# Value tiles of 96 rows, split over 8 DMA engines instead of 16

## The chip, the cores and the metric

The kernel runs on one core of a Trainium2 chip. The core has a matrix engine (TensorE, PE in the profile, with its weight loads as PEld), VectorE (DVE), ScalarE (ACT), GpSimd (POOL) and SyncE (SP), which here issues the DMAs, and 16 DMA engines that carry them out. What counts is the time of one launch on the device in microseconds (us), as the median of several runs.

## The reference

Four sequences of 768 tokens with 8 heads of 64 pass through windowed attention with summaries, and the result through a layer with a gate:

```python
k_sum = k.reshape(B, H, nb, block, D).max(axis=3)        # block 32: 24 summaries
v_sum = v.reshape(B, H, nb, block, D).mean(axis=3)
mask_l = np.abs(pos[:, None] - pos[None, :]) < window     # window 16
scores_l = scale * (q @ k.T)                              # masked by mask_l
scores_s = scale * (q @ k_sum.T) + np.log(block)
a = softmax(concatenate([scores_l_masked, scores_s]))
x = a @ concatenate([v, v_sum])                           # tokens x 512
h = x @ w_in                                              # 512 -> 2048
out = (h * erf(softplus(h))) @ w_out                      # 2048 -> 512
```

All inputs and the output are float32.

## The kernel before, in words

The 3072 tokens are six chunks of 512. A chunk and a pair of heads make a *quad*, 24 in all. For attention a quad is cut into eight blocks of 64 queries; a block needs 96 keys and values around it and the 24 summaries of its sequence, so a block's product of probabilities and values runs over 120 rows: the 96 rows of a value tile, and 24 rows of value summaries below them. The value tile of a quad is `vw`, [120 rows, 8 blocks, 128 columns]; its 96 rows come by one DMA from the DRAM array `v_win` (a row is 8 x 128 floats, 4096 bytes, 384 KB in all), and its other 24 rows by a DMA from the tile `vsum`, where the summaries lie once. The product is called px in the profile (line 663, function `av`).

The gated layer is cut into 24 periods, six chunks by four groups of hidden columns. In each period TensorE makes h for one group (`mm1`, in later periods `products`, which saves multiplications by sums of blocks of the weights), ScalarE and VectorE make softplus, erf and the gate, and `mm2` adds the group's part of the output. Products are made in pieces of a rounded high part and a low part, which need three passes. The attention of later quads is placed between them: `load_quad` brings queries and keys, `load_quad_v` the value tile, about a period before `av` uses it.

The first chunk is special. Its four quads (pairs 0 to 3) have value tiles of their own, `vwf`, two pairs in one buffer, loaded by `load_vw_first` (line 493), and the rows of the summaries come from `vsum_first`: pair 0's by a copy on ScalarE, pairs 1 to 3 by DMAs (line 510). Between these loads SyncE issues the first weight loads `rw` (line 314, 1024 KB each), which VectorE converts from 64-bit to 32-bit floats. TensorE fills some gaps there with products of zeros (`idle`, line 958), a fixed number of them.

What sets the order: the program adds every piece of work to a plan with its engine, an assumed duration and what it reads and writes. `P.order` then runs the plan through once, with a table `TUNE` of added numbers by piece, and so writes down a fixed order for each engine. All loads are SyncE's. A DMA gets one of eight completion semaphores in turn, and SyncE doesn't issue a DMA before the one that is eight before it on that semaphore has landed; it also waits for whoever last used the buffer.

On the host, `kernel` cuts the windows of the values out of `v` and lays them down as `v_win`, [6 chunks, 4 pairs, 96 rows, 8 blocks, 128 columns]. What is done on the host isn't part of the time.

Of the kernel before, what the change touches and what calls it, by code (L numbers as in the profile page):

```python
# [23 lines left out]
NP = H // 2  # L24
T = 512
SB = S // 64
NB = T // 64
# [3 lines left out]
LW = 96  # L31
NK = LW + NS
NCH = B * S // T
# [147 lines left out]
def bfloat16(x):  # L181

    n = np.array([x], np.float32).view(np.uint32)
    return float(((n + 0x8000) & 0xFFFF0000).astype(np.uint32).view(np.float32)[0])
# [3 lines left out]
def block_attention_mlp(ctx: ExitStack, tc: tile.TileContext, q_t, k_nat, k_win, v_tok, v_nat, v_win, w_in, w_out, out):  # L188
    nc = tc.nc
# [7 lines left out]
    def sb(shape, dtype, name, tag=None):  # L197

        n = math.prod(shape[1:])
        if n % 128 == 0:  # L200
            return pool.tile(shape, dtype, name=name, tag=tag or name)
        t = pool.tile([128, -(-n // 128) * 128], dtype, name=name, tag=tag or name)[0:shape[0], 0:n]
        return t if len(shape) == 2 else t.rearrange("p (a b) -> p a b", a=shape[1]) if len(shape) == 3 else t.rearrange("p (a b c) -> p a b c", a=shape[1], b=shape[2])
# [31 lines left out]
    for i in range(3):  # L235
        c = bfloat16(rest)
# [37 lines left out]
    def dma(kb, fn, r=(), w=(), hold=2.0, **kw):  # L274
        return P.add({"SP": max(0.45, kb / 350.0)}, lambda e: fn(), r, w, hold=hold, **kw)
# [196 lines left out]

    st = {}

    def where(qd):

        ch, p = divmod(qd, NP)
        seqs = {}
        for j in range(NB):
            seqs.setdefault((NB * ch + j) // SB, []).append(j)  # L480
        return ch, p, [(b, slice(js[0], js[-1] + 1)) for b, js in seqs.items()]
# [8 lines left out]
            dma(786, lambda n=n: nc.sync.dma_start(out=vts[n], in_=v_tok[3 * n:3 * n + 3].rearrange("t s c -> s t c")), w=[f"vt{n}"])  # L490

    def load_vw_first(p):
        dma(585, lambda: nc.sync.dma_start(out=st[p]["vw"][0:LW], in_=v_win[0, p]), w=[f"vwf{p}"])

    def ksum_first(p):
        on({"DVE": 0.86}, lambda e: e.tensor_reduce(ksum[:, 0, p], groups(kfirst[p]), op=ALU.max, axis=AX.X), [f"kf{p}"], [f"ksum0{p}"])
# [16 lines left out]
    def load_quad(qd):  # L513
        ch, p, seqs = where(qd)
        s = st[qd] = {}

        def go_q():
            s["qb"] = sb([128, T], F32, "qb")
            nc.sync.dma_start(out=s["qb"], in_=q_t[ch, p])

        def go_k():
            s["kw"] = sb([128, NB, NK], F32, "kw")
            nc.sync.dma_start(out=s["kw"], in_=k_win[ch, p])
        dma(262, go_q, w=["qb"])
        dma(465, go_k, w=["kw"])
        for b, js in seqs:
            n = js.stop - js.start
            on({"DVE": 0.06 + 0.025 * n, "ACT": 0.2 + 0.018 * n}, lambda e, b=b, js=js, n=n: copy(e, s["kw"][:, js, LW:NK], ksum[:, b % 2, p:p + 1, :].to_broadcast([128, n, NS])),
               [f"ksum{b % 2}{p}"], ["kw"])

    def load_quad_v(qd):
        ch, p, seqs = where(qd)
        s = st[qd]

        def go():
            s["vw"] = sb([NK, NB, 128], F32, "vw")
            nc.sync.dma_start(out=s["vw"][0:LW], in_=v_win[ch, p])
        dma(585, go, w=["vw"])
        for b, js in seqs:
            n = js.stop - js.start  # L540
            dma(100 if n == NB else 50, lambda b=b, js=js, n=n: nc.sync.dma_start(out=s["vw"][LW:NK, js], in_=vsum[vrows[b % 2], p:p + 1, :].to_broadcast([NS, n, 128])),
                [f"vsum{b % 2}{p}"], ["vw"])
# [422 lines left out]
    for p in range(NP):  # L965
        load_vw_first(p)
# [69 lines left out]
    for k in range(NPER):  # L1036
        qa, qs = k + NP, k + NP + 1
        ch, g = divmod(k, NG)
# [169 lines left out]
```

## Time and profile before

| | |
|---|---|
| median of 3 runs | 622.92 us (621.27 to 622.95) |
| profiled execution, its own time | 622.58 us |
| its span, first to last instruction | 620.8 us |
| TensorE busy | 612.9 us, 99% |
| VectorE, ScalarE busy | 424.0 us, 422.3 us (68% each) |
| granted TensorE clock | 1.000 |
| DMA | 150.25 MB in 36845 packets, mean 242 GB/s |
| of it v_win | 24 tiles of 384 KB |

The page cuts the span into 40 slices of some 15.5 us and gives the busy share of each engine in tenths:

```profile
PE   9999999999999999999999999999999999999997
DVE  4989999975989886766857646548546556425442
DMA  8999868654784698799767776756786654574612
GB/s 321 256 337 354 287 205 283 250 183 172 247 304 184 236 339 309 244 370 319 240 217 245 234 264 232 257 209 216 266 289 219 225 170 181 210 265 162 246 68 69
```

TensorE reads 9 in nearly all slices; the DMA engines' 9s are in the first few. A busy TensorE is not the same as a full one, and filling products with zeros count as busy too. In the views that follow, a row of the chain or the timeline begins with the start and the length in us; a row of waits names the engine and line that waited, what it waited for, the sum in us, how often, and the longest.

### The profile page before, as it was taken

The page shows a single profiled execution, that of the slowest core. Times are in us where ns is not written, and L with a number is a line of the kernel's source. Part 1 is how long each engine was busy: PE and PEld are TensorE (multiplying, and loading weights), DVE is VectorE, ACT ScalarE, POOL GpSimd, SP SyncE. Part 2 cuts the span into 40 slices and gives each one's busy share as a digit, 9 for nine tenths or more (in the row PEclk, how much of TensorE's full clock was granted, in tenths as well). Part 3 has the DMA queues.
Part 4 walks back from the last instruction along what each step waited for, and adds up shares of the span by engine and source line. Part 5 has one row for each costly group of instructions (what it writes and reads, how often), then busy time and mean ns, then how long its engine had stood idle before and what let it go on. Part 6 is the DMA issues. An engine that isn't in the chain of part 4 may idle for free.

```text
span 620.8 us, 12141 instructions
## 1 busy us (share of the span) xinstructions
PE 612.9 (99%) x4786; PEld 514.4 (83%) x4786; DVE 424.0 (68%) x884; ACT 422.3 (68%) x855; POOL 3.7 (1%) x27
## 2 busy tenths in 40 slices
PE   9999999999999999999999999999999999999997
PEld 5676666888788889989889889899898898899886
DVE  4989999975989886766857646548546556425442
ACT  5869988986879786885866854855756655552450
POOL 2000000000000000000000000000000000000000
PEclk9999999999999999999999999999999999999999
DMA  8999868654784698799767776756786654574612
GB/s 321 256 337 354 287 205 283 250 183 172 247 304 184 236 339 309 244 370 319 240 217 245 234 264 232 257 209 216 266 289 219 225 170 181 210 265 162 246 68 69
DMA packets 36845, 150.25 MB, mean 242 GB/s; under 512 B 3956, under 2 KB 9396, under 8 KB 24244
## 3 DMA queue, kind: packets, MB, share of 16 engines
q1 hardware_dynamic: 36212, 148.95, 69.4%
q8 instruction: 38, 0.62, 0.4%
q10 hardware_dynamic: 576, 0.52, 0.2%
q14 instruction: 19, 0.16, 0.1%
HBM read 124.13 MB, written 23.07 MB: 237 GB/s over the span
## 4 chain that ended last, share of the span: by engine, by line
PE 93%; DMA 6%; SPq 0%; issue 0%; DVE 0%; ACT 0%
PE ops L921 39%; PE hb L807 15%; PE h L766 13%; PE ha L807 11%; PE ops L917 4%; PE px L663 4%; PE pA L566 3%; DMA rw<-w_in 2%; DMA vwf<-vsum 2%; PE pA L637 1%; PE pB L637 1%; DMA vt<-v_tok 1%; PE pB L566 0%; PE vt L460 0%; SPq L485 0%; SPq L486 0%
## 5 line engine op out<-in xcount | busy, mean ns | idle before, releaser
L921 PE MATMUL ops<-w,gh 128*128 128x512 f32 x704 | 232.8, 396 | 0.0
L921 PEld LDWEIGHTS ops<-w,gh 128*128 128x128 f32 x704 | 132.5, 188 | 27.9 <-issue 0.6
L921 PE MATMUL ops<-w,gl 128*128 128x512 f32 x352 | 137.3, 390 | 0.0
L1166 ACT ACT_TABLE_LOAD x87 | 111.6, 1283 | 1.5
L897 DVE TENSOR_TENSOR hc<-wt,hc 128x1024 f32<-128x1024 f32 x44 | 53.3, 1220 | 76.5 <-ACT wt L885 76.5
L766 PE MATMUL h<-xh,w 128*128 128x512 f32 x256 | 88.8, 406 | 0.0
L278 ACT COPY hc<-hb 128x256 f32<-128x256 f32 x61 | 22.7, 373 | 96.2 <-DVE hc L860 47.6
L921 PEld LDWEIGHTS ops<-w,gl 128*128 128x128 f32 x352 | 66.3, 188 | 12.0
L606 ACT ACTIVATE pr<-pr,stats 128x120 f32<-128x120 f32 x160 | 60.9, 383 | 0.2
L766 PEld LDWEIGHTS h<-xh,w 128*128 128x128 f32 x256 | 48.1, 188 | 12.3 <-issue 2.1
L807 PE MATMUL hb<-w,ws 128*128 128x256 f32 x384 | 56.3, 283 | 0.0
L904 DVE TENSOR_TENSOR gl<-hc,gh 128x1024 fp32r<-128x1024 f32 x44 | 53.8, 1222 | 1.6 <-ACT gh L278 0.7
L807 PEld LDWEIGHTS hb<-w,ws 128*128 128x128 f32 x384 | 50.7, 192 | 0.1
L885 ACT ACTIVATE wt<-wt 128x1024 f32<-128x1024 f32 x48 | 50.4, 1061 | 0.4
L766 PE MATMUL h<-xl,w 128*128 128x512 f32 x128 | 49.9, 390 | 0.0
L857 DVE TENSOR_TENSOR hc<-hb,hc 128x256 f32<-128x256 f32 x32 | 13.5, 422 | 37.4 <-PE hb L807 36.4
L278 DVE CAST gh<-hc 128x1024 fp32r<-128x1024 f32 x38 | 26.3, 691 | 18.1 <-PE ops L921 17.1
L873 ACT ACTIVATE wt<-hc 128x1024 f32<-128x1024 f32 x32 | 32.4, 1052 | 0.2
L606 ACT ACTIVATION_READ_ACCUMULATOR pr<-pr,stats 128x1 f32 x160 | 30.0, 187 | 0.0
L917 PE MATMUL ops<-a32s,gw 128*128 128x512 f32 x64 | 29.5, 595 | 0.0
L766 PEld LDWEIGHTS h<-xl,w 128*128 128x128 f32 x128 | 24.1, 188 | 5.6 <-issue 1.2
L807 PE MATMUL ha<-w,ws 128*128 128x256 f32 x192 | 28.3, 283 | 0.0
(162 smaller groups left out, 1033.9 us busy)
## 6 DMA issues: line engine op xcount, KB each, us to landing
w<-dr SPq DMA_DIRECT2D x36, 1024.0 KB
ws<-ds SPq DMA_DIRECT2D x30, 1024.0 KB
kw<-k_win SPq DMA_DIRECT2D x20, 480.0 KB
rw<-w_in SPq DMA_DIRECT2D x8, 1024.0 KB
rw<-w_out SPq DMA_DIRECT2D x8, 1024.0 KB
dr<-w SPq DMA_DIRECT2D x8, 1024.0 KB
ds<-ws SPq DMA_DIRECT2D x8, 1024.0 KB
vw<-v_win SPq DMA_DIRECT2D x20, 384.0 KB
```

The lines of the kernel that those rows point to most:

```text
L278: e.copy(o, i) if e is nc.scalar else e.tensor_copy(o, i)
L606: nc.scalar.activation(s["pr"][:, j], s["pr"][:, j] if qd >= MQ else s["sc"][j // NI][:, i * NK:(i + 1) * NK], AF.Exp, scale=-1.0 if qd >= ...
L663: nc.tensor.matmul(xo[r, o], lhsT=s["vw"][:, j, r], rhs=s["pt"][:, a, o], start=True, stop=True)
L766: nc.tensor.matmul(hs[k, f][:, 0:T], lhsT=w[m], rhs=xt[ch, cc][x], start=(cc == 0 and n == 0), stop=(cc == 3 and n == 2))
L807: nc.tensor.matmul(shape, lhsT=w[m], rhs=y[l], start=first and c == 0 and i == 0, stop=c == 1 and i == 2, skip_group_check=True)
L873: nc.scalar.activation(wt[k, n], hc[k, n], AF.Softplus)
L885: act(0.96, lambda n=n: nc.scalar.activation(wt[k, n], wt[k, n], AF.Erf, scale=-1.0 if k < SOFT else 1.0), [s], [s], table=("sig",), after ...
L897: e.tensor_tensor(hc[k, n], wt.pop((k, n)), hc[k, n], op=ALU.mult)
L904: e.tensor_tensor(gs[k, n][1], hc.pop((k, n)), f32(gs[k, n][0]), op=ALU.subtract)
L917: nc.tensor.matmul(os_[ch, t], lhsT=x[0][:, i % 2, t * 128:(t + 1) * 128], rhs=w32["o", g, i // 2][:, i % 2], start=first, stop=last)
L921: nc.tensor.matmul(os_[ch, t], lhsT=x[y][:, i % 2, t * 128:(t + 1) * 128], rhs=w[m], start=first and n == 0, stop=last and n == 2)
L1166: nc.scalar.preload_act_table_set(sets[o["load"]])
```

## The change

The 96 rows of a tile lie in DRAM as 8 groups of 12 rows, and after each group there is room for a thirteenth row that is never read. The source of the DMA thus has the three sizes 8, 12 and 1024 instead of 96 and 1024, and can't be joined into one run of 96 rows. The destination in the chip's memory, the bytes, the length of a row and the place in SyncE's order are the same. All 24 loads of `v_win` are changed, the four of the first chunk and the twenty of the others. The first size, 8, is what is meant to set over how many DMA engines a transfer is split.

```diff
+    def eight(ch, p):
+        return v_win[ch, p, :, 0:12].rearrange("e r (j c) -> e r j c", c=128)
...
     def load_vw_first(p):
-        dma(585, lambda: nc.sync.dma_start(out=st[p]["vw"][0:LW], in_=v_win[0, p]), w=[f"vwf{p}"])
+        dma(585, lambda: nc.sync.dma_start(out=st[p]["vw"][0:LW], in_=eight(0, p)), w=[f"vwf{p}"])
...
             s["vw"] = sb([NK, NB, 128], F32, "vw")
-            nc.sync.dma_start(out=s["vw"][0:LW], in_=v_win[ch, p])
+            nc.sync.dma_start(out=s["vw"][0:LW], in_=eight(ch, p))
...
-    v_win = np.ascontiguousarray(windows(v).transpose(0, 2, 4, 1, 3, 5)).reshape(NCH, NP, LW, NB, 128)
+    v_win = np.zeros((NCH, NP, 8, 13, NB * 128), dtype=f)
+    v_win[:, :, :, :12] = windows(v).transpose(0, 2, 4, 1, 3, 5).reshape(NCH, NP, 8, 12, NB * 128)
```

## The prediction

> **What bounds the kernel now.** I read first the page's busy line, then stretches of the span, then TensorE's own waits, then the chain that ended last, and last the queue of DMAs in the stage that these left over. The page and two rows of the stretches (busy time of PE, PEld, DVE, ACT, POOL, then the granted clock, DMA share, GB/s):
>
> ```profile
> PE 612.9 (99%) x4786; PEld 514.4 (83%) x4786; DVE 424.0 (68%) x884; ACT 422.3 (68%) x855; POOL 3.7 (1%) x27
> 0.00:40.00 40.00, 35.57 (x485) 23.56 (x486) 28.96 (x48) 26.45 (x91) 3.69 (x27) 1.00 0.97 287
> 40.00:100.00 60.00, 60.00 (x384) 39.59 (x385) 59.11 (x109) 51.68 (x92) 0.00 (x0) 1.00 0.83 293
> ```
>
> TensorE is busy in 60.00 of the 60.00 us from 40 on, at the full clock (1.00); the 4.4 us that it misses early lie in the first 40 us, where the DMA engines are busy 0.97 of the time. So the kernel has two parts: a start bound by DMA, and a rest bound by TensorE. TensorE's waits and the chain (start, length, what) agree:
>
> ```profile
> PE px L663 <- DMA vwf<-vsum: 2.1, 2, 1.1
> PE px L663 <- ACT prf L626: 0.5, 1, 0.5
> PE px L663 <- issue: 0.4, 1, 0.4
> ...
> 2.60 7.28 DMA vt<-v_tok
> 9.90 15.35 DMA rw<-w_in
> 25.26 14.56 DMA vwf<-vsum
> 39.83 0.14 issue
> 39.97 1.15 PE px L663 x32
> ```
>
> The chain runs through DMAs up to 39.83 and through TensorE from 39.97. That last px (pair 3's product with the value tile) needs pair 3's 96-row v_win tile and the 24-row copy from vsum that is issued behind it. After it no px waits for a value tile: the rows above are all the waits that a px has, and none names vw.
>
> **The queue of the start.** These are SyncE's issues of the four v_win tiles and of pair 3's copy, and the weight loads (rw, 1024 KB) between them:
>
> ```profile
> 6.42 0.43 SPq L314 DMA_DIRECT2D rw<-w_in  x1
> 7.59 0.34 SPq L493 DMA_DIRECT2D vwf<-v_win  x1
> 9.90 0.34 SPq L314 DMA_DIRECT2D rw<-w_in  x1
> 10.89 0.33 SPq L493 DMA_DIRECT2D vwf<-v_win  x1
> 21.82 0.52 SPq L314 DMA_DIRECT2D rw<-w_in  x1
> 22.39 0.42 SPq L493 DMA_DIRECT2D vwf<-v_win  x1
> 22.86 0.43 SPq L314 DMA_DIRECT2D rw<-w_in  x1
> 23.33 0.81 SPq L493 DMA_DIRECT2D vwf<-v_win  x1
> 25.26 0.83 SPq L510 DMA_DIRECT2D vwf<-vsum  x1
> ```
>
> All four tiles stand ahead of the copy that lands at 39.83, 14.56 us after its issue. The queue is backed up, so what an engine carries for the tiles delays everything behind them. The rate in stretches:
>
> ```profile
> 10.00:15.00 5.00, 4.92 (x79) 2.86 (x79) 2.50 (x7) 4.01 (x24) 0.00 (x0) 1.00 1.07 417
> 15.00:20.00 5.00, 4.96 (x82) 2.90 (x81) 4.97 (x11) 4.94 (x28) 0.00 (x0) 1.00 1.02 292
> 20.00:25.00 5.00, 4.55 (x53) 3.17 (x52) 5.00 (x9) 4.95 (x20) 0.00 (x0) 1.00 1.06 233
> 25.00:30.00 5.00, 3.95 (x50) 3.08 (x49) 4.96 (x7) 2.80 (x5) 0.00 (x0) 1.00 1.02 257
> 30.00:35.00 5.00, 4.48 (x48) 3.55 (x46) 3.89 (x7) 3.87 (x11) 0.00 (x0) 1.00 1.03 281
> 35.00:40.00 5.00, 3.97 (x28) 3.09 (x24) 3.98 (x5) 2.61 (x4) 0.00 (x0) 1.00 1.02 277
> 40.00:45.00 5.00, 5.00 (x49) 4.08 (x50) 4.97 (x6) 2.86 (x5) 0.00 (x0) 1.00 1.02 409
> 23.00:27.00 4.00, 3.54 (x33) 2.67 (x32) 3.96 (x6) 3.88 (x15) 0.00 (x0) 1.00 1.09 159
> 34.00:38.00 4.00, 3.99 (x49) 3.59 (x50) 2.94 (x4) 2.41 (x4) 0.00 (x0) 1.00 1.04 243
> ```
>
> With the engines always busy, tiles of 128 rows come at 417 and 409 GB/s, but the 25 us in which 96-row and 24-row tiles run among them come at a mean of 268 (292, 233, 257, 281, 277). By bytes 25 x (1 - 268/417) = 8.9 us are lost there. I take this as tiles of other row counts getting in the way of their neighbours; the trace shows the rate, not the cause.
>
> **The change, part by part.** Nothing on TensorE, VectorE, ScalarE or GpSimd is added or moved, and the order of SyncE's issues stays.
>
> (1) *The split itself.* How many engines take part shows in the small packets, one per engine and DMA:
>
> ```profile
> DMA packets 36845, 150.25 MB, mean 242 GB/s; under 512 B 3956, under 2 KB 9396, under 8 KB 24244
> w<-dr SPq DMA_DIRECT2D x36, 1024.0 KB
> ...
> vw<-vsum SPq DMA_DIRECT2D x12, 96.0 KB
> vw<-vsum SPq DMA_DIRECT2D x16, 48.0 KB
> vwf<-vsum SPq DMA_DIRECT2D x3, 96.0 KB
> ```
>
> The view lists 255 DMAs; 255 x 16 = 4080, and 4080 - 3956 = 124 = 31 x 4, so the 31 copies of 24 rows run on 12 engines and all others on 16. The split follows the leading size, so 8 groups should give 8. I expect 24 x 8 = 192 small packets fewer, 3764.
>
> (2) *Four tiles in the start.* A tile is 384 KB: 24,576 bytes an engine now, 49,152 on each of eight engines then. The extra 24,576 bytes take 0.94 us at the full rate (417/16 = 26.1 GB/s an engine) and 1.47 us at the stage's (268/16 = 16.8). Four tiles stand ahead of pair 3's copy: +3.8 to +5.9 us. The other eight engines get ahead by as much, but a landing waits for the last engine, and what they then find queued is what stands behind the tiles. The earlier px at 27.90 and 34.01 move by part of this sum; they are not added, since the last one contains them.
>
> (3) *What the smaller spread gives back.* Only eight engines write a 96-row tile at a time, so there may be less of the 8.9 us loss. The copies from vsum aren't touched: 23 to 27 us, where they run, loses 4 x (1 - 159/417) = 2.5 us alone, and half of the 1.7 us of 34 to 38 is likewise theirs. At most some 5.6 us are the v_win tiles'. The ends are then 3.8 - 5.6 = -1.8 and +5.9 us. I take +3.8: the full-rate price, with the loss neither smaller nor larger. For a change in the loss there is no row that shows it, and twelve rows on eight engines keep as many rows of the tile beside the other engines' weight rows, only for longer.
>
> [...]
>
> (4) *Who pays.* TensorE ends its work ahead of pair 3's px soon after the last row here that precedes it, and then idles:
>
> ```profile
> 27.90 1.15 PE L663 MATMUL px<-ptr,vwf 120*64 120x64 f32 x32 [1.05 <-DMA vwf<-vsum]
> 34.01 1.15 PE L663 MATMUL px<-ptr,vwf 120*64 120x64 f32 x32 [0.52 <-ACT prf L626]
> 38.55 0.39 PE L766 MATMUL h<-xh,w 128*128 128x512 f32 x1
> 39.97 1.15 PE L663 MATMUL px<-ptr,vwf 120*64 120x64 f32 x32 [1.03 <-DMA vwf<-vsum]
> ```
>
> So there is no slack in front of a later landing: the px starts 0.14 us after it. And with TensorE fully busy from 40 us on there is none behind: every microsecond goes to the end. VectorE waits for weight loads in this stage too (row below); those land later by fewer tiles, so its shift is smaller than the px's and is hidden behind it.
>
> ```profile
> DVE a L331 <- DMA rw<-w_in: 2.1, 2, 1.0
> L541 SPq DMA_DIRECT2D vw<-vsum x28: 785/827/883, 63.0 to 499.7; - x28
> L537 SPq DMA_DIRECT2D vw<-v_win x20: 328/337/728, 53.6 to 494.3; - x20
> ```
>
> (5) *The issue.* The new pattern has a size more than the old, like the copies', whose issue takes 827 ns where a v_win issue takes 337. Per tile that is 0 to +0.49 us on SyncE. I take 0: the tiles at 22.39 and 23.33 are queued behind work of many microseconds. Uncovered, four would cost 2.0 us.
>
> (6) *Twenty later tiles.* Each is slower by 0.94 to 1.47 us on its engines. I take 0, covered by TensorE's work: no px waits for vw. Uncovered, all twenty would cost up to 29 us; one alone, 1.5.
>
> The profiled execution's time is 622.58 us with a span of 620.8, so 1.8 lie around it; it is 0.34 under the median, 622.92. The sum is 622.58 + 3.8 = 626.4, or **626.7** against the median.
>
> **The rivals.** *No measurable change*: the loss shrinks by about what the eight engines carry more, 1.9 to 5.6 us, and the copy lands between 1.8 us earlier and 1.9 us later: 621.1 to 624.8. The dips in the rate speak for it, the untouched vsum copies against it. In this I also count that the DMAs still run on 16 engines, against the count of small packets: 622.9.
>
> *Larger loss*: the eight engines meet neighbours as often per byte as now. From 15.0 us an engine carries four rw (65,536 each), four tiles and three copies (8,192 each), 385,024 bytes, 14.8 us at the full rate, and takes 24.8 (to 39.83), a factor 1.68. With 483,328 bytes: 18.5 x 1.68 = 31.1 us, 6.3 later: 629.2. For it speaks that the slow stretches hold nearly the whole stage; against it, fewer engines in the tile.
>
> *Faster*: the v_win tiles stop disturbing the weight loads altogether, and TensorE's waits before px go: 1.05 + 0.52 + 1.03 and the 0.4 of issue, 3.0 us at most: 619.9. It decides from the point where pair 3's copy lands before 38.0 us. Against it: the second of these waits belongs to ScalarE, and the 5.6 us would have to go entirely.
>
> *A late tile in the TensorE part*: a px after 40 us begins to wait for vw, 1 to 2 us for each that does, on top of the forecast: 628 to 630. Against it stands that no such wait exists now.
>
> **How the numbers follow.** Forecast (a landing 1.9 to 5 us later, 624.8 to 628): 0.41. Larger loss 0.19; no measurable change 0.28, of which 0.03 for no split; faster 0.07; a late tile 0.05. A measurement of this kernel tells 0.3%, 1.87 us, from no change: 621.05 to 624.79 is the same. So slower 0.65, same 0.28, faster 0.07. The range leaves out the faster case, the early edge of the no-change case and the worst of the larger loss: 621.7 to 630.0; the forecast's own is 624.8 to 628.
>
> **What would show it.** The split: 3764 packets under 512 B. Term 2: the last px on vwf starts near 43.8 instead of 39.97, with a wait of some 4 to 5 us for DMA vwf. Term 3: the rate from 15 to 40 us; near 268 GB/s or a little under bears the forecast out, over 300 the no-change or the faster case. Term 4: busy 60.00 of 60.00 after the shifted px. Term 5: the issue of v_win near 827 ns. Term 6: no row of a px waiting for vw. I am wrong if the copy lands before 41.7 us, or if the end moves by other than the last px does.

## The result, and the profile after

Over 14 runs each, the kernel after takes 624.8 us in the median (622.97 to 630.25) and the kernel before 622.34 (621.11 to 623.23). The ratio is 1.0056, with an interval from 1.0036 to 1.0076: slower by 3.5 us, with 2.2 to 4.7 as bounds. The ratio is that of the means (625.72 and 622.22 us); the medians lie only 2.5 us apart, since six of the 14 runs after are over 626 and pull the mean up. The profiled execution takes 627.37 us with a span of 625.6, which is 4.8 more than the span before, so it lies on the upper side of the runs. What follows is used for where the time goes; how much goes is taken from the runs.

The page after, its busy line and its packets:

```profile
PE 615.0 (98%) x4786; PEld 516.0 (82%) x4786; DVE 424.7 (68%) x884; ACT 422.0 (67%) x855; POOL 3.7 (1%) x27
DMA packets 36653, 150.25 MB, mean 240 GB/s; under 512 B 3764, under 2 KB 9204, under 8 KB 24052
```

The same instructions and the same bytes; 192 small packets fewer (3956 before), as one per engine and DMA gives when 24 tiles go from 16 engines to 8. TensorE's products of pairs 0 to 3 with their value tiles, in order of time (start, length, what, and in brackets how long TensorE stood idle ahead of it and for what):

```profile
22.15 1.62 PE L666 MATMUL px<-ptr,vwf 120*64 120x64 f32 x32
28.42 1.15 PE L666 MATMUL px<-ptr,vwf 120*64 120x64 f32 x32 [1.31 <-DMA vwf<-vsum]
37.11 1.98 PE L666 MATMUL px<-ptr,vwf 120*64 120x64 f32 x32 [3.08 <-DMA vwf<-v_win]
44.74 1.15 PE L666 MATMUL px<-ptr,vwf 120*64 120x64 f32 x32 [1.16 <-DMA vwf<-vsum]
```

Before, the last three started at 27.90, 34.01 and 39.97. The lag is 0.52, then 3.10, then 4.77 us: it grows from tile to tile, and what it is at the last of them is what the span is longer by. A wait that did not exist before has the largest part, pair 2's product waiting for its own 96 rows. The chain of waits names the same place; its last DMA is pair 3's copy, issued at 24.81 and landed at 44.61 (before: 25.26 and 39.83).

```profile
24.81 19.80 DMA vwf<-vsum
```

Stretches of the kernel after (busy us of PE, PEld, DVE, ACT, POOL, then the granted clock, the DMA share, GB/s):

```profile
20.00:25.00 5.00, 4.85 (x56) 3.55 (x56) 5.00 (x10) 4.92 (x19) 0.00 (x0) 1.00 0.75 238
25.00:30.00 5.00, 3.59 (x48) 2.49 (x46) 5.00 (x7) 2.73 (x8) 0.00 (x0) 1.00 1.05 264
30.00:35.00 5.00, 4.02 (x18) 2.98 (x16) 2.96 (x7) 4.40 (x12) 0.00 (x0) 1.00 1.03 258
35.00:40.00 5.00, 2.89 (x37) 2.81 (x38) 2.70 (x4) 0.88 (x2) 0.00 (x0) 0.71 1.02 278
15.00:40.00 25.00, 20.32 (x234) 14.55 (x233) 20.62 (x32) 17.91 (x66) 0.00 (x0) 0.94 0.97 267
45.00:100.00 55.00, 55.00 (x320) 35.83 (x319) 52.57 (x88) 47.81 (x85) 0.00 (x0) 1.00 0.75 271
```

Two things are new. From 20 to 25 us the DMA engines are busy 0.75 of the time, where before they were busy throughout (1.06). And from 35 to 40 the granted clock is 0.71. What is not new is the rate over the whole stretch from 15 to 40 us: 267 GB/s after, 268 before. From 45 us on TensorE is busy without a gap (575.00 of the 575.00 us to 620), and no px waits for a later value tile.

### The profile page after: what moved, and what is told of

Its sections match the earlier page's. It is cut to its first block, busy times and chain, and to the rows that moved or that the text cites. A ratio compares the mean times of both kernels' runs of the same rounds, so it can differ in the third digit from the quotient of the medians.

```text
span 625.6 us, 12141 instructions
## 1 busy us (share of the span) xinstructions
PE 615.0 (98%) x4786; PEld 516.0 (82%) x4786; DVE 424.7 (68%) x884; ACT 422.0 (67%) x855; POOL 3.7 (1%) x27
## 2 busy tenths in 40 slices
DMA packets 36653, 150.25 MB, mean 240 GB/s; under 512 B 3764, under 2 KB 9204, under 8 KB 24052
## 4 chain that ended last, share of the span: by engine, by line
PE 94%; DMA 3%; ACT 1%; SPq 1%; DVE 0%; issue 0%
PE ops L924 39%; PE hb L810 15%; PE h L769 13%; PE ha L810 11%; PE ops L920 4%; PE px L666 4%; DMA vwf<-vsum 3%; PE pA L569 3%; PE pA L640 1%; PE pB L640 1%; ACT prf L609 1%; PE idle L961 1%; PE pB L569 0%; PE vt L460 0%; SPq L513 0%; SPq L496 0%
## 5 line engine op out<-in xcount | busy, mean ns | idle before, releaser
L278 ACT CAST xh<-px 128x512 fp32r<-128x512 f32 (+1 forms) x17 | 8.9, 524 | 32.1 <-PE px L666 28.8
```

The lines of the kernel that those rows point to most:

```text
L278: e.copy(o, i) if e is nc.scalar else e.tensor_copy(o, i)
```

## The experiments

The theory (A) was the prediction's: in the start the eight engines that carry a v_win tile carry twice its bytes, four such tiles stand ahead of pair 3's copy, and the last px and the end move by that. Its rivals: (B) the later twenty tiles cost something; (C) the pattern itself costs, its gaps or its issue; (D) fewer engines at one tile give something back. The changed line numbers of variants are those of their own code. "Faster" and "slower" are against the kernel before, run on the same chip.

### Which tiles: the first four, or the later twenty

Both lay the DRAM tile out as 104 rows. One kernel reads the gapped form for chunk 0 alone; the other, with `False` in place of `True`, for all chunks but 0. The edit of the host's part, which fills the rows to match, is left out here:

```
-        return v_win[ch, p, :, 0:12].rearrange("e r (j c) -> e r j c", c=128)
+        if (ch == 0) == True:
+            return v_win[ch, p].rearrange("(e r) x -> e r x", r=13)[:, 0:12].rearrange("e r (j c) -> e r j c", c=128)
+        return v_win[ch, p, 0:LW].rearrange("r (j c) -> r j c", c=128)
```

> Only the four value tiles of the first chunk lie in 8 groups of 12 rows; the other twenty are read as 96 rows, as before. Theory A (the start): the eight engines' extra rows ahead of pair 3's copy set the end, the later tiles are covered by TensorE. It expects the whole loss here: +2.5 to +4.5 us against before, the last px on vwf at 42.5 to 45, 3956 - 32 = 3924 packets under 512 B. Theory B (the later tiles cost, by disturbing the weight loads or by a late vw) expects less than half of it, under +1.7 us.

> The other part alone: the four first tiles are read as 96 rows, the twenty later ones in 8 groups. Theory A (the start) expects no change, within 1 us of before, the last px on vwf near 40 and no px that waits for vw. Theory B (the later tiles) expects +1.7 us or more. Packets under 512 B: 3956 - 160 = 3796.

With the first four alone: 625.91 us, a ratio of 1.0057 (1.0036 to 1.0079), which is the whole loss of the change. With the later twenty alone: 622.27 us, 0.9998 (0.9986 to 1.0009). The products of pairs 1 to 3 in the one, and then pair 3's in the other:

```profile
29.16 1.98 PE L668 MATMUL px<-ptr,vwf 120*64 120x64 f32 x32 [2.57 <-DMA vwf<-vsum]
37.52 1.15 PE L668 MATMUL px<-ptr,vwf 120*64 120x64 f32 x32
43.47 1.15 PE L668 MATMUL px<-ptr,vwf 120*64 120x64 f32 x32 [1.02 <-DMA vwf<-vsum]
```

```profile
40.02 1.15 PE L668 MATMUL px<-ptr,vwf 120*64 120x64 f32 x32 [0.97 <-DMA vwf<-vsum]
```

Pair 3's product starts 3.5 us later than before in the one, with a span 3.5 longer (624.3 against 620.8), and at 40.02 with the span of before (620.8) in the other. Which of the earlier products takes the longest wait differs between the two traces (pair 1's here, pair 2's in the kernel after); the lag at pair 3 is what counts. B falls: whatever the twenty tiles cost on their engines (0.94 us each and more by the prediction's estimate) vanishes behind TensorE's work.

### How many engines: 16, 12, 8, 4

The same gapped layout with other group sizes; the function `eight` reads rows `0:6`, `0:8` or `0:24` of a group instead of `0:12`:

```
-    v_win = np.zeros((NCH, NP, 8, 13, NB * 128), dtype=f)
-    v_win[:, :, :, :12] = ...reshape(NCH, NP, 8, 12, NB * 128)
+    v_win = np.zeros((NCH, NP, 16, 7, NB * 128), dtype=f)      # or 12, 9 / 4, 25
+    v_win[:, :, :, :6] = ...reshape(NCH, NP, 16, 6, NB * 128)  # or 12, 8 / 4, 24
```

> All 24 tiles lie in 16 groups of 6 rows with a gap of one row: the pattern with three sizes, the gaps and the longer issue stay, the number of engines goes back to 16. Theory A (rows per engine in the start) expects no change, within 1 us of before, and 3956 packets under 512 B. Theory C (the pattern, the gaps or the issue of about 0.74 us instead of 0.34 cost the time, not the number of engines) expects the whole loss, +2.5 to +4.5 us.

> All 24 tiles lie in 12 groups of 8 rows, so that 12 engines take 8 rows each, two more than before. Theory A (rows of the busiest engine ahead of pair 3's copy): 4 tiles x 2 rows x 4096 bytes at 26.1 to 16.8 GB/s, +1.3 to +2.0 us. [...] Packets under 512 B: 3956 - 24 x 4 = 3860.

> All 24 tiles lie in 4 groups of 24 rows, so that four engines take 24 rows each, 18 more than before instead of 6. Theory A says that the loss goes with the rows of the busiest engine: 4 tiles x 18 rows x 4096 bytes at 26.1 GB/s is +11.3 us, at the slow rate of the stage (16.8 GB/s) +17.6; it expects +9 to +14 us, the last px on vwf at 49 to 54. Theory D (the loss comes from collisions on the way into the 96 rows, which become fewer the fewer engines write) expects less than twice the loss with 8 groups, under +6 us. Packets under 512 B: 3956 - 24 x 12 = 3668.

Small packets were 3956, 3860 and 3668, so these tiles ran on 16, 12 and 4 engines. The price by the forecast's term is the bytes that the busiest engine carries more over four tiles, at the 26.1 GB/s that each moved from 10 to 15 us before (417/16):

| engines | rows on the busiest | bytes more, four tiles | at 26.1 GB/s | measured (interval) |
|---|---|---|---|---|
| 16, with gaps | 6 | 0 | 0 | +0.1 us (-0.7 to +0.9) |
| 12 | 8 | 32,768 | 1.3 us | +0.6 us (-0.6 to +1.7) |
| 8 (the change) | 12 | 98,304 | 3.8 us | +3.5 us (2.2 to 4.7) |
| 4 | 24 | 294,912 | 11.3 us | +13.4 us (12.5 to 14.5) |

The first row takes C away: the gaps and the additional size of the pattern cost nothing that can be measured. The twelve-engine run does not decide between A and no price at all; its profiled execution (624.8 us of span, px of pair 3 at 43.95) was at the upper end of its runs, which go from 620.94 to 626.58. The last row is the largest effect of the study, and it is where the term says, in the waits for value tiles:

```profile
33.06 1.97 PE L666 MATMUL px<-ptr,vwf 120*64 120x64 f32 x32 [5.57 <-DMA vwf<-vsum]
42.51 1.15 PE L666 MATMUL px<-ptr,vwf 120*64 120x64 f32 x32 [1.70 <-DMA vwf<-v_win]
51.53 1.97 PE L666 MATMUL px<-ptr,vwf 120*64 120x64 f32 x32 [4.08 <-DMA vwf<-vsum]
```

In this trace pair 3's product starts 11.56 us later than before (51.53 against 39.97), next to the 11.3 of the term. The span is 13.0 us longer, so 1.4 us are lost behind that product, where the granted clock was 0.50 until about 54.9 us. So the measured loss, with an interval from 12.5, lies above 11.3, but the lag at the last product is the term's; what is lost behind it was not in the forecast.

D falls as an explanation of the total: no layout was faster than 16 engines. The rates are against it too. From 15 to 40 us the twelve-engine kernel moved 245 GB/s, less than the 268 of the kernel before, while 16 groups of six rows moved 301:

```profile
20.00:25.00 5.00, 4.60 (x56) 3.36 (x55) 5.00 (x10) 4.95 (x20) 0.00 (x0) 1.00 0.82 189
15.00:40.00 25.00, 22.56 (x270) 16.50 (x270) 23.75 (x35) 19.20 (x65) 0.00 (x0) 1.00 0.98 301
```

That row says one thing more: 33 GB/s above the kernel before in the mean of this stretch, and no gain in the time (+0.1 us). The rate of a stretch is not the landing that is waited for. The packet counts give how many engines a DMA ran on (16, 12, 8 and 4, and 12 for the 24-row copies). That four such tiles meet the same engines each time, as the sum of the term takes it, was the author's estimate; no row here shows which engines they were, but the prices in the table fit a sum over four tiles.

### Does the clock make it worse?

After the wait of 3.08 us the granted clock was 0.50 for some 3.4 us (37.1 to about 40.5), and the px itself took 1.98 us instead of 1.15. To see what that costs, the four-engine kernel, where the waits are longest, was given products with a zero operand ahead of the products of pairs 1 to 3, so that TensorE never stood idle for long:

```
-FILL = {30: 3, 48: 2, 79: 1, 81: 6, 93: 5, 91: 1, 111: 1}
+FILL = {30: 3, 48: 2, 79: 1, 81: 6, 93: 5, 91: 1, 111: 1, 86: 22, 95: 8, 104: 15}
```

> The kernel with 4 groups of 24 rows (635.56 us), with products of zeros put ahead of px 1, 2 and 3 (22, 8 and 15 of them, some 0.22 us each), so that TensorE does not sit idle there. In the run without them the granted clock was 0.50 for 3 to 3.5 us after the waits of 5.57 and 4.08 us, and the span grew by 13.0 us although the last px moved by 11.6. If the lower clock costs the difference, the clock stays at 1.00 and the time falls by 1 to 2 us, to 633.5 to 634.5. If the wait alone counts, the time stays at 635.6 or grows.

```profile
51.53 1.15 PE L666 MATMUL px<-ptr,vwf 120*64 120x64 f32 x32 [1.07 <-DMA vwf<-vsum]
```

The product takes 1.15 again and the mean clock is 1.00, but it starts at the same 51.53, and the time is 635.45 us against 635.56. The expectation of a gain was wrong: up to the last px, work at half the clock was finished before the next tile landed anyway. The span of this one execution is 0.8 us shorter, all of it behind the last px, but the medians of four runs each do not show it.

With eight engines no such run was made, but the clock is not the whole loss there either. Of the 14 runs after, two had a mean clock of 1.000 and took 624.05 and 624.83 us, 1.8 and 2.6 us over the mean of the kernel before. The six runs over 626 us all had 0.997 or less. Whether the lower clock makes those longer, or only comes with longer waits, is not shown.

### Is it SyncE, held at the copies?

The dip to 0.75 suggested another theory. SyncE issues its DMAs in order, and stands at the first copy from vsum until vsum is there, at about 20.4 us (a wait of 8.9 us); the weight loads of the start wait behind it, the next of them until 22.18 us. With 16 engines the queue of the kernel before held enough for all (1.06); with eight, the engines without v_win rows may have run dry, so that what the others carry could not be covered. A row above already speaks against it: the kernel with 16 groups had a dip too, to 0.82 in the same five microseconds, and no loss. If the theory were true, the loss would go when the copies leave SyncE's queue. This theory is H. First GpSimd made the copies itself, in the kernel before and in the kernel after:

```
-                dma(100, lambda p=p: nc.sync.dma_start(out=st[p]["vw"][LW:NK], in_=vsum[LW:NK, p:p + 1, :].to_broadcast([NS, NB, 128])), ...)
+                dma(100, lambda p=p: copy(nc.gpsimd, st[p]["vw"][LW:NK], vsum[LW:NK, p:p + 1, :].to_broadcast([NS, NB, 128])), ...)
```

> The kernel before (96 rows on 16 engines), but the three copies of 24 rows from vsum into the first value tiles are made by GpSimd, which is idle, instead of by DMAs; the orders of the other engines stay. If the copies cost the queue what the prediction took from the rate (2.5 us at 23 to 27 us and some 0.8 later), the last px on vwf comes earlier, up to what TensorE's waits allow: -1 to -2.6 us, with a rate from 15 to 40 us near 300 GB/s. SyncE also no longer waits there for vsum, which works the same way. If the slow rate is the 96-row tiles' alone, within 1 us of before and a rate near 268.

> The same copies by GpSimd, with the tiles in 8 groups of 12 rows. If the copies' cost and the eight engines' rows simply add, the loss of the changed kernel shrinks by some 3 us: -1 to +1 us against before. If the eight engines' rows alone set the landing of the last tile, the loss stays: +2 to +4 us, and the last px waits for v_win itself.

With 16 engines 623.15 us, a ratio of 1.0012 (1.0000 to 1.0024); with eight 623.32, 1.0016 (1.0007 to 1.0026). So the loss of the eight engines is all but gone, 0.2 us between the two. But three things had changed at once: SyncE is free, the three DMAs are gone, and VectorE is slower while GpSimd works beside it. GpSimd's copies and one of VectorE's instructions under them, and then the same instruction in the kernel before:

```profile
20.34 3.50 POOL L278 COPY vwf<-vsum 24x1024 f32<-24x1024 f32 x3 [14.73 <-ACT vsum L505]
22.85 2.06 DVE L334 SCALAR_TENSOR_TENSOR a<-rw,a 128x1024 uint32<-128x1024 uint32 x1
```

```profile
21.09 1.22 DVE L334 SCALAR_TENSOR_TENSOR a<-rw,a 128x1024 uint32<-128x1024 uint32 x1
```

VectorE was busy 24.59 of the 25 us from 15 to 40 in the one with 16 engines, 22.80 before. The instruction has the same shape in both and took 2.06 us beside GpSimd's copies against 1.22; the next of that shape, behind them, took 1.23 again. By what it was slowed is not shown. To take the three apart, the copies stayed DMAs and went to GpSimd's queue, with every other engine's order as it was:

```
-                dma(100, lambda p=p: nc.sync.dma_start(out=...
+                dma(100, lambda p=p: nc.gpsimd.dma_start(out=...
```

> The changed kernel (8 groups of 12) with the three copies of vsum into the value tiles of pairs 1, 2 and 3 issued as DMAs from GpSimd's queue instead of SyncE's; nothing else moves: TensorE, VectorE and ScalarE run the same rows in the same order, SyncE has two rows of vsum fewer ahead of the w_in and v_win transfers. In the kernel after, SyncE stood at these copies until vsum was ready at about 20.4 us, and in 20-25 us the DMA share was 0.75. Theory H (while SyncE is held, the eight engines without v_win rows run dry, so that the rows that the other eight have to carry can't lie beside other transfers): DMA share in 20-25 us at 0.95 or more, rate over 15-40 us at 290 GB/s or more (267 in the kernel after), no wait of TensorE for v_win over 1 us, px of pair 3 at 39.5 to 41.5, and a time within 0.2% of the kernel before. Rival Q (the eight engines are simply late by their rows, whoever issues the copies): the copies are no longer waited for, but px of pair 2 or 3 still waits 2 us or more for v_win, the rate stays at 265 to 280, and the kernel is slower than before by 0.3 to 0.6%. Rival G (a third: a copy on another queue is served in turn with the large transfers and comes late): TensorE waits 1 us or more for DMA vwf<-vsum, and the kernel is slower than before by 0.2% or more.

> The kernel before (96 rows over 16 engines) with the three copies of vsum issued from GpSimd's queue; the same on TensorE, VectorE and ScalarE. The waits that this can take away are those of px for DMA vwf<-vsum in the kernel before, 1.05 and 1.03 us. Theory H: the rate over 15-40 us rises from 268 GB/s to 290 or more, px of pair 3 is at 38.5 to 39.5, and the kernel is faster than before by 0.05 to 0.3% (621.0 to 622.3). Rival Q: the rate stays below 280, px of pair 3 at 39.5 to 40.5, no change in the time. Rival G: a wait for DMA vwf<-vsum remains that is as long as before or longer, and the kernel is the same or slower by up to 0.3%.

With eight engines 625.98 us, 1.0069 (1.0047 to 1.0090, six runs); with 16, 622.78, 1.0007 (0.9993 to 1.0020). The loss is back in full. Stretches with eight engines, TensorE's wait there, and then the longer stretch with 16:

```profile
20.00:25.00 5.00, 4.37 (x50) 2.86 (x48) 4.93 (x10) 4.95 (x20) 1.98 (x3) 1.00 1.04 310
15.00:40.00 25.00, 21.16 (x245) 15.54 (x243) 21.04 (x33) 19.04 (x65) 1.98 (x3) 1.00 1.02 283
```

```profile
PE px L666 <- DMA vwf<-v_win: 3.7, 2, 2.4
```

```profile
15.00:40.00 25.00, 21.43 (x245) 15.45 (x243) 22.11 (x33) 19.25 (x65) 2.01 (x3) 1.00 1.02 277
```

The DMA share is 1.04 now where it was 0.75, so the queue is no longer held; and the products of pairs 2 and 3 still wait 3.7 us, now for the v_win tiles alone. H falls: the dip is real, but it is not the price. The granted clock was 1.00 throughout this stretch, and pair 3's product started at 42.79, so this execution also shows the lag without a lower clock. Rival Q holds, the tiles are late by their own rows, with a rate just above the 280 and a loss just above the 0.6% that it allowed. Rival G has something too: with 16 engines pair 1's product waited 2.0 us for its copy, which may be why the free SyncE brought nothing there. One reservation: the move changed the copies as well as their queue. The three of them are 144 packets on GpSimd's queue, and were 612 on SyncE's.

### What hid the loss in GpSimd's case

Two things were left: the three DMAs are gone, or VectorE was so slow that late tiles did not matter. ScalarE made the copies this time, as it does for pair 0, so that GpSimd and VectorE are as before:

```
+                dma(100, lambda p=p: copy(nc.scalar, st[p]["vw"][LW:NK], vsum[LW:NK, p:p + 1, :].to_broadcast([NS, NB, 128])), ...)
```

> The kernel before (96 rows over 16 engines) with the three copies of vsum for pairs 1, 2 and 3 made by ScalarE (as pair 0's is, 1.04 us each) instead of three DMAs; GpSimd does nothing, TensorE and VectorE run the same rows in the same order, two of the copies stand ahead of pair 1's copies out of PSUM on ScalarE. Theory V (the three copies as DMAs, 512 bytes a piece, take about 25 GB/s of the start whoever issues them: 277 GB/s over 15-40 us with them on GpSimd's queue, 300 without): rate over 15-40 us at 295 GB/s or more, px of pair 3 at 38.5 to 39.7 without a wait for DMA, time 0.05 to 0.25% under the kernel before. Rival Q (the copies as DMAs cost the rate little; GpSimd's copies had slowed VectorE and so left the transfers more time): rate 265 to 285, px of pair 3 at 39.5 to 41, time within 0.15% of the kernel before.

> The same edit on the changed kernel (8 groups of 12), where GpSimd's copies had left a loss of 0.2 us against the same edit with 16 engines, and copies by DMA from GpSimd's queue one of 3.5 us. Theory V: rate over 15-40 us at 300 GB/s or more, TensorE waits for v_win 1.5 us in all or less, px of pair 3 at 39 to 41, and the loss against the same edit with 16 engines is 0.25% or less. Rival Q (the loss of the eight engines was only hidden behind a VectorE that GpSimd had slowed): px of pair 2 or 3 waits 2 us or more for v_win, and the loss against the same edit with 16 engines is 0.4 to 0.7%.

With 16 engines 622.7 us, 1.0009 (1.0000 to 1.0017); with eight 623.17, 1.0018 (1.0007 to 1.0028): a loss of 0.1%, 0.5 us, between the two. TensorE's longest wait, then the stretches, then pair 3's product, with 16 engines:

```profile
PE pA L637 <- ACT ptr L642: 1.5, 1, 1.5
```

```profile
20.00:25.00 5.00, 4.14 (x50) 2.81 (x49) 5.00 (x10) 4.94 (x19) 0.00 (x0) 1.00 1.02 302
25.00:30.00 5.00, 3.53 (x49) 2.37 (x46) 3.18 (x4) 4.18 (x7) 0.00 (x0) 1.00 1.02 283
30.00:35.00 5.00, 5.00 (x39) 3.78 (x40) 4.96 (x8) 4.88 (x12) 0.00 (x0) 1.00 1.02 277
35.00:40.00 5.00, 5.00 (x63) 4.14 (x59) 4.41 (x6) 3.65 (x5) 0.00 (x0) 1.00 1.00 390
15.00:40.00 25.00, 22.62 (x268) 16.04 (x268) 22.52 (x34) 22.60 (x68) 0.00 (x0) 1.00 1.02 312
```

```profile
39.26 1.23 PE L663 MATMUL px<-ptr,vwf 120*64 120x64 f32 x32
```

The same three views with eight engines:

```profile
PE pA L640 <- ACT ptr L645: 1.8, 1, 1.8
```

```profile
20.00:25.00 5.00, 4.50 (x52) 3.04 (x51) 5.00 (x9) 4.92 (x20) 0.00 (x0) 1.00 1.02 306
25.00:30.00 5.00, 3.19 (x39) 2.21 (x39) 3.15 (x5) 4.20 (x6) 0.00 (x0) 0.91 1.03 329
30.00:35.00 5.00, 5.00 (x28) 4.03 (x25) 4.91 (x8) 4.35 (x11) 0.00 (x0) 0.75 1.01 313
35.00:40.00 5.00, 5.00 (x54) 4.11 (x53) 3.20 (x5) 3.31 (x6) 0.00 (x0) 1.00 1.02 313
15.00:40.00 25.00, 22.64 (x242) 16.30 (x242) 21.23 (x34) 21.75 (x67) 0.00 (x0) 0.93 1.02 312
```

```profile
40.78 1.23 PE L666 MATMUL px<-ptr,vwf 120*64 120x64 f32 x32
```

In neither does a product wait for a DMA any more, and the rate is 312 GB/s in both, against 277 with the copies as DMAs on a free queue. So VectorE's slowness is not needed to hide the loss, and theory V has the transfers right: without the three copies as DMAs, the eight engines' rows land before they are asked for. As an estimate, the copies cost the start 25 x (1 - 277/312) = 2.8 us of its rate; with those given back, a lag of 3.5 us has nearly all its cover, and 0.5 us of it are left.

Two things limit this. The 16-group layout above moved 301 GB/s with all three copies on SyncE's queue, so the layout of the tiles alone moves the rate about as much as the copies do, and the 2.8 us are not a price of the copies that would hold elsewhere. And in both of these kernels TensorE now waits for ScalarE ahead of pair 1's product (1.5 and 1.8 us), because two of the copies stand before the work that it needs; how much of the lag that wait covers is not shown. In the profiled executions pair 3's product is 1.5 us later with eight engines, more than the medians differ; that one ran part of the time from 25 to 35 us at a lower clock (0.91 and 0.75).

On the time V missed: it expected the 16-engine kernel to gain 0.05 to 0.25%, and it gained nothing, although the last px starts 0.71 us earlier than before. From that start to the end of the span there are 581.44 us; in the kernel before, in the kernel after and in the runs with the first four, the later twenty, 16 and 12 groups there are 580.78 to 580.86. So 0.6 of the 0.7 us were lost again behind it, and TensorE's wait for ScalarE (1.5 us) stands where waits for DMA had been. Nothing tried was faster than the kernel before.

## Why the prediction was right, step by step

**What bounds the kernel** held: what the start loses at pair 3's product is lost for the whole. In the profiled execution the product is 4.77 us later and the span 4.8 longer.

**Term 1, the split,** was exact: 3764 small packets.

**Term 2, four tiles in the start,** was right in its place and nearly in its size. Term +3.8, measured +3.5 (2.2 to 4.7), by the ratio; in medians the kernel is 2.5 us slower, and 624.8 us lies 1.9 under the 626.7 forecast, of which 0.6 is that the kernel before came out at 622.34 this time instead of 622.92. The full-rate price was the better end to take: the upper end, by the stage's rate, was +5.9, outside the interval. At four engines the same two ends are 11.3 and 17.6 us, and the last product was 11.56 us later. But the choice of that end was partly luck: by the prediction's own words no row stood behind it. Single executions also scatter around the term: the lag at pair 3 was 4.77 us in the kernel after, 3.50 with the first four alone, and 3.98 with twelve engines, where the term says 1.3.

**Term 3, what the smaller spread gives back,** was taken as nothing, and over the start no change of the rate was seen: 267 GB/s against 268. These are single executions; kernels with the same loads in the start gave 274 (the first four alone) and 265 (the later twenty alone), so a change of less than some 10 GB/s would not be seen. How it comes to nothing the forecast could not say, and no run tests it. Where no copies disturb it, the eight-engine kernel moves more from 20 to 35 us (306, 329 and 313 GB/s against 302, 283 and 277) and less after (313 against 390), and by 40 us the same, 312 GB/s in both; that would fit tiles that disturb their neighbours less and last longer, which is a guess. Fewer engines at a tile did not raise the rate by themselves: 8 rows on each of twelve engines moved 245 GB/s, six rows on 16 engines 301. For the copies from vsum the prediction had some 3.3 us of lost rate; the estimate from ScalarE's copies is 2.8, with the limits given there.

**Term 4, who pays,** held in its main claim: the px of pair 3 starts 0.14 us after its copy lands, and the lag goes to the end in full. One detail was wrong. The sign that was given, a wait of some 4 to 5 us at pair 3, did not come: that wait was 1.16 us, hardly more than before (1.03). Most of the lag had built up by pair 2, whose product waited 3.08 us for its v_win rows and started 3.10 us late.

**Term 5, the issue:** 737 ns in the median where 827 was expected and 337 was the price before.

```profile
L540 SPq DMA_DIRECT2D vw<-v_win x20: 707/737/753, 58.4 to 499.1; - x20
```

It costs nothing, as taken: the 16-group layout, whose later tiles took 660 ns to issue, has no loss. **Term 6, the later tiles:** nothing, as taken; the kernel with the later twenty alone shows it.

**The rivals.** *No measurable change* came nearest: its upper edge was 624.8, which is the forecast's lower edge and just where the median fell. That there is a change rests on the interval of the ratio, on the first four alone (1.0036 to 1.0079) and on the four-engine kernel, not on where that median lies. What this rival needed, a loss that shrinks by the eight engines' extra, does not show in the bytes by 40 us. *Larger loss*, 629.2, is at the upper end of single runs (630.25) but not of the median. *Faster* would have needed pair 3's copy before 38.0; it landed at 44.6. *A late tile in the TensorE part* did not occur. What the prediction did not see at all is that the clock falls to 0.50 behind some of the waits and that the runs spread: over 7 us after, 2 before.

## What to carry to other kernels

In this kernel, transfers that are confined to fewer DMA engines were priced by the rows on the busiest engine, summed over all such transfers that stand ahead of the one that is waited for, and paid only in the stage where that landing is waited for: four tiles of 24 made the whole loss, twenty cost nothing, and with three copies fewer in the queue most of the price was covered. So look first for the landing that is waited for, and for what stands ahead of it. The mean rate over a stage does not show the price (267 against 268 GB/s with a loss, 301 without a gain); the start of the product that waits last does. And a dip in the DMA share beside a loss is not its cause until the dip has been taken away: here it went, and the loss stayed.

## What the runs showed of the hardware beside this

The granted clock of TensorE was halved around many of the longer waits. In the kernel after, behind the wait of 3.08 us:

```profile
37.00:38.00 1.00, 0.89 (x17) 0.93 (x19) 0.47 (x1) 0.00 (x0) 0.00 (x0) 0.55 0.87 205
38.00:39.00 1.00, 1.00 (x21) 0.89 (x18) 0.00 (x0) 0.00 (x0) 0.00 (x0) 0.50 0.98 244
40.00:41.00 1.00, 1.00 (x7) 0.96 (x6) 0.75 (x2) 1.00 (x2) 0.00 (x0) 0.75 1.11 281
41.00:42.00 1.00, 1.00 (x6) 0.82 (x5) 1.00 (x2) 0.63 (x2) 0.00 (x0) 1.00 0.96 237
```

It was 0.50 too at waits of 2.57, 4.08 and 5.57 us, and a px took 1.97 or 1.98 us each time. The length of the wait does not decide it. With twelve engines the longest wait was 2.24 us, and the clock was halved behind it:

```profile
25.00:30.00 5.00, 2.90 (x21) 2.10 (x20) 3.86 (x6) 2.63 (x7) 0.00 (x0) 1.00 1.01 237
30.00:35.00 5.00, 4.86 (x42) 4.07 (x43) 3.21 (x6) 3.27 (x8) 0.00 (x0) 0.66 1.02 257
```

Behind one of 2.40 us (eight engines, copies on GpSimd's queue) it stayed at 1.00. One long wait isn't needed either. With eight engines and GpSimd's own copies no wait of TensorE in the start was over 1.6 us, but it worked only 1.06 of 3.30 us, and then:

```profile
25.00:28.30 3.30, 1.06 (x8) 0.88 (x9) 3.30 (x6) 1.82 (x3) 0.00 (x0) 0.96 1.02 361
28.30:30.00 1.70, 1.70 (x32) 1.70 (x32) 1.70 (x2) 0.00 (x0) 0.00 (x0) 0.50 1.04 248
```

The halved clock lasted some 3.4 us here (37.1 to about 40.5), behind the 4.08 us (51.4 to 54.9) and with twelve engines (a mean of 0.66 from 30 to 35 us). It lasted twice as long, 6.8 us, at the waits of 2.57 us (28.5 to 35.4) and 5.57 us (31.0 to 37.8), where an expectation above says 3 to 3.5. A stretch that was busy for a third, and waits of 2.24 and 2.57 us, had it behind them, the wait of 2.40 us had not; what sets it off, and for how long, is not shown. In the one run that took the low clock away the time stayed the same (635.45 us against 635.56).

The other surprise is how far the rate of the start moves. The three small copies inside SBUF are 0.3 of the 7.8 MB that moved from 15 to 40 us in the kernels with ScalarE's copies. Without them as DMAs the rate there was 300 to 316 GB/s in four kernels. With them it was 265 to 283 in six kernels whose tiles ran on 16 or eight engines, 245 with twelve engines, 235 and 239 with four. The exception is the layout in 16 groups, with 301. Each is one execution, and why that layout is faster is not known.
